# A gated mix of attention and a dense layer on one core: four two-reading sets whose sum GpSimd makes, eleven tiles of powers, and a new order

## The chip, the cores and the metric

The kernel runs on one core of one Trainium2 chip. A core has a matrix engine (TensorE, PE in the profile), a vector engine (VectorE, DVE), an engine for activation functions (ScalarE, ACT), a programmable engine (GpSimd, POOL) and SyncE (SP), which here only issues transfers between the DRAM and the core's on-chip memory. Each engine runs its own instructions in order, and they wait for each other by semaphores. The metric is the time of one execution on the device, in microseconds (us); less is better.

## The reference

`x` is 2048 rows of 640 values in bf16. A gate g is computed for each row, and the result mixes an attention `a` over 32 heads of 20 values and a dense layer `b`, both of the shape of x:

```python
x = A_x
g = _sigmoid((x * gate_w).sum(-1, keepdims=True))
# a: q, k, v = x @ wqkv in 32 heads; softmax(q k^T / sqrt(20)) v; @ wo
a = _A_ref(x, A_wqkv, A_wo)
# b: h = x @ w1 + b1 (1536 wide); h * tanh(softplus(h)); @ w2
b = _B_ref(x, B_w1, B_b1, B_w2)
return g * a + (1 - g) * b
```

The bulk is the softmax: 32 heads x 2048 x 2048 scores, each of which needs an exponential, and a product with the values.

## The kernel before, in words

**Groups.** The heads are taken four at a time (8 head groups p), the queries 512 at a time (4 chunks qc): 32 groups G. In each group the 2048 keys are 16 tiles j of 128, and a tile has four units, one for each head. A unit's scores are one matmul that uses 32 rows of PE (`score`, L1074), so four units of different heads can run at the same time; they fill one bank of PSUM, the accumulator memory of eight banks. Seven banks hold scores and other results, the eighth (`acc`) gathers the products with the values.

**Two ways to an exponential.** Of most tiles ACT makes the exponentials (`emit_exp`, L1092), mostly of two banks at once. Of 167 tiles, here called sets, DVE makes powers instead: `power_of` (L587) multiplies a bank's scores, adds a constant and writes 16-bit integers, whose bits read as bf16 are a rough exponential, into a quarter of a tile `T` of 128x2048. The roughness is averaged out by several readings of the same powers: GpSimd adds a constant to every 16-bit integer (`add_shift`, L617, an INT64_ADD that treats four of them as one word), which makes another tile, and the value product is made with each reading.

- An ordinary set (`d_shifts`) has three readings: T and two shifted ones. PE makes three value steps `V j,0`, `V j,1`, `V j,2` with them, the second and third with values scaled beforehand (`VD`).
- A two-reading set (`d_sum`) has a shifted tile, to which T is added (`total`, L641), and T shifted in place (`again`). PE makes two value steps. Six sets of the kernel before are of this kind, and DVE makes their sum.

T tiles have numbered places, T0 to T8 before: nine tiles for powers and shifted ones.

**The dense work.** Projections, the layer b and the product with wo are `Chain`s of column matmuls (`product`, L664), cut in pieces. Weights of the q and k projections come in strips (`load_strip`, L433), w1 in pairs of columns (`load_w1`, L446). The attended rows go to DRAM and come back transposed as `od` (`load_o`, L924). Twice ACT runs Mish over half of b's hidden values (`mish`, L872) for 10.4 us; PE works on chains in that time.

**The order.** Nothing is scheduled when the kernel is built. A string, `ORDER`, lists 5820 steps, and the loop at the end of the kernel emits them one by one; an engine's order is that in which its instructions come from the string. The letters that matter here:

- `S n,k`: n units of scores for ACT into banks k and on; `x n`: the exponential of n of these banks
- `d G,tag,two`: a set of group G is taken from the end of its keys, its T at place tag; `two` says of which kind it is
- `D G,j,r,k`: scores of unit r of the set (G, j) into bank k; `y n`: the n-th of DVE's waiting steps, a power, a copy out of PSUM or a sum
- `p n,tag`: the n-th of POOL's waiting steps, its output at place tag (-1: none, or in place)
- `V j,i`: the value step of key tile j with reading i (-1: ACT's exponentials), of the group that is being gathered
- `C`, `F`: begin a chain, make its next piece; `H`: filler matmuls; `q`, `k`, `b`, `o`, `l`: transfers on SP's queue; `m`: Mish

POOL's steps are numbered when they become known: a set's shifts once its last power is emitted.

Of the kernel before, what the change touches and what calls it, by code (L numbers as in the profile page):

```python
# [19 lines left out]
C0,4 S2,5 S2,2 S2,0 x2 x2 F F F F F C1,5 F y1 y3 C2,6 F x2 y4 C3,5 S2,2 F x2 y5 S2,0 C4,6 F x2 y2 y6 S2,2 C6,5  # L20
x2 F F F F F F F F F F F F F F F F F F F F C5,6 F F S2,0 S2,3 F F F x2 y7 y8 y9 x2 y10 y11 y12 C7,2 F F F F F
S2,0 x2 S2,5 C8,3 F F F F F F F F F F F F F F d1,3,0 V0,-1 F F F F F F V1,-1 y13 y14 y15 x2 C9,4 S3,0 F F F F
S2,5 F x3 x2 y16 y17 y18 y19 C10,6 V2,-1 S3,1 V4,-1 V3,-1 S2,4 V5,-1 F F F F F x3 x2 y20 C11,5 S3,0 d0,8,0 F F
d1,1,0 F F F F F F F F F F D0,15,3,4 D0,15,0,3 F F F F F F F F C12,6 V6,-1 x3 S3,0 F F F F y21 y23 y24 d0,0,0
y22 y25 y26 y27 x3 S2,3 D0,15,2,5 F x2 y28 y29 S3,0 C13,5 V7,-1 F F S2,3 D0,14,3,6 F F F x2 q1 y30 y31 x1 x2
C14,0 V9,-1 S2,1 D0,15,1,6 F F F F F F F F F D0,14,0,3 S2,4 F F F V8,-1 y32 x2 q2 y33 x2 D0,14,1,6 S2,1 F F F
F F F F F y34 x2 y35 C15,6 V10,-1 S3,3 y36 y37 y38 y39 F F F F F F D0,14,2,2 v0,0 S2,0 V15,0 F F F F V11,-1 x3
y41 y42 y40 p1,2 x2 D1,15,1,5 S3,2 y43 y44 x3 V14,0 V15,1 y45 D1,15,0,6 y46 C16,5 S2,0 V12,-1 F F F F F F
d1,2,0 D1,15,2,6 S3,2 p3,4 p4,7 p2,6 l0 y47 F V14,1 F F F V13,-1 x2 x3 D1,14,0,6 S2,0 d2,5,0 y48 y49 y50 V14,2
V15,2 C17,5 F x2 D1,15,3,4 S2,2 d1,0,0 y51 l1 F F x2 y52 D1,14,1,6 S2,0 d2,4,0 F F x2 p5,6 S2,2 D1,14,2,4 x2  # L30
p6,8 y54 y55 y56 l2 V0,-1 V1,-1 C18,5 S2,0 D1,13,0,6 F F F x2 y57 y53 y58 S3,2 F F S2,0 D1,13,1,6 V15,0 V2,-1
V15,2 V15,1 x3 y59 l3 y60 x2 D1,12,0,5 y61 C19,6 S3,2 F F F F F F V3,-1 S2,0 D1,14,3,5 F d2,6,0 F F F x3 y62
V4,-1 S3,2 x2 l4 y63 p7,7 y64 q3 x1 x2 C21,2 V5,-1 V14,0 D1,13,3,6 S2,0 D2,15,0,5 F F F F p8,8 y65 y66 x2
D1,13,2,6 S2,3 l5 y67 V14,1 F x2 D1,12,3,5 S2,0 y68 p9,3 V14,2 V13,0 V6,-1 x2 y69 D1,12,2,6 S3,2 p10,1 y70 x1
l6 x2 C20,2 V7,-1 V13,1 d3,7,0 D1,12,1,5 S2,0 y71 x2 F F F F F F F F F D2,15,3,6 S3,3 F V12,0 V13,2 V8,-1
p11,3 y72 x3 l7 p12,8 y73 V12,1 S2,0 D2,15,1,6 y74 y75 x2 C22,2 V9,-1 F F D2,14,0,3 S2,4 F F F F D2,15,2,6
S2,0 F F F F y76 x2 l8 y77 x2 y78 S2,3 y79 x2 C23,6 D2,14,3,5 V12,2 F F V10,-1 D2,14,1,0 S2,1 F V11,-1 F y80
p13,3 d2,2,1 y81 x2 l9 y82 S2,3 D2,13,0,5 F F F F F S2,0 D2,14,2,2 F p14,0 x2 y84 x2 y83 y85 V15,2 S2,4
D2,13,3,3 V15,1 V0,-1 D2,13,1,2 S2,0 p15,8 x2 e0 p16,3 x2 y86 y87 y89 y90 e2 V1,-1 V15,0 C24,2 V14,0 V14,1
S2,3 D2,12,0,5 F F S2,0 D2,13,2,6 F F x2 y91 x2 D2,12,3,5 S2,3 d2,1,0 x2 y92 y93 p17,8 V2,-1 d3,0,0 F S2,0  # L40
D2,12,1,6 V3,-1 V13,0 V14,2 y94 x2 p18,5 y95 D2,11,0,4 S2,2 x2 C25,5 V13,1 F S2,0 D2,12,2,6 F F y96 y88 y97 x2
D2,11,3,4 S2,2 F F p19,4 y98 x2 S2,0 D2,11,1,6 y99 x2 y101 V4,-1 V13,2 S2,2 d3,3,0 C26,5 D3,15,0,4 F F F S2,0
D2,11,2,6 F V6,-1 y102 x2 S2,2 D3,15,3,4 F V5,-1 y100 x2 y103 y105 x2 p20,-1 q4 S2,0 V12,0 V7,-1 x2 y104
d3,8,0 p21,6 D3,14,0,6 S2,2 D3,14,3,5 V11,0 V12,1 y106 x2 S2,0 D3,15,1,4 p22,5 y107 x2 y108 V11,1 C27,5 V8,-1
D3,13,0,6 S2,2 F F F F F D3,15,2,4 S2,0 F F F F F y109 x2 y110 k1 x2 D3,13,3,6 S2,2 x2 y111 d3,6,0 y113 p23,2
y112 V11,2 V9,-1 S2,0 D3,14,1,4 V10,-1 C29,6 x2 d3,4,0 y114 F F S2,2 D3,12,0,5 F F p24,1 y115 x2 D3,14,2,4
S2,0 V15,0 F y116 x2 d4,5,0 y117 y118 y119 S2,2 D3,12,3,5 V15,1 V0,-1 p25,7 x2 S2,0 D3,13,1,4 y121 y122 V14,0
V15,2 D3,11,0,6 S2,2 V14,1 V1,-1 x2 p26,2 y123 x2 D3,13,2,5 D3,12,1,4 S2,0 y120 y124 x2 V14,2 V2,-1 C28,6 F F
F F F F F q5 y125 S2,2 D3,11,3,5 p27,2 S2,0 y126 x2 F F F p28,1 y127 x2 y128 v1,0 V3,-1 V13,1 V13,0 C30,6 S3,2
D3,10,0,5 F F F F F x1 x2 y130 y131 y129 y132 D3,10,3,5 S3,0 x1 d4,2,0 x2 C34,0 d4,0,0 V4,-1 V13,2 V5,-1 S2,3  # L50
D3,12,2,6 F F F y133 y134 x2 D4,15,0,5 S2,1 p29,7 y135 F F x2 y136 p30,3 V12,0 S2,3 D3,11,1,6 V6,-1 V12,1 x2
y137 S3,0 D3,11,2,5 V12,2 x1 y138 S2,3 D3,10,2,6 x2 y139 C31,0 d4,1,0 V7,-1 F v2,0 F F d5,7,0 p31,8 x2 S2,1
D3,10,1,6 D4,14,0,5 q6 p32,3 x2 V11,0 F S2,3 F V8,-1 V11,1 y143 y142 p33,6 x2 y144 D4,15,1,6 S2,1 D4,13,0,5
V10,0 V11,2 p34,8 y145 x2 S2,3 D4,15,2,0 y146 x2 y147 C32,5 V9,-1 V10,1 D4,14,1,6 S2,1 F V10,2 y148 x2 S2,3
D4,15,3,0 F F S2,1 D4,13,1,6 F F y149 x2 y150 x2 p35,6 S2,3 D4,14,2,0 V0,-1 V15,0 V1,-1 y151 y152 y154 x2 S2,1
D4,12,0,6 p36,3 x2 y155 y153 C33,5 F d4,4,0 V2,-1 F S2,3 D4,14,3,0 x2 V15,2 V15,1 S2,1 D4,12,1,6 F F F x2 y141
y157 y140 p37,8 D4,13,2,0 S2,3 V3,-1 V14,0 y158 y160 y159 x2 S2,1 D4,11,0,6 p38,5 y161 y156 x2 C35,0 V14,1
V4,-1 D4,13,3,5 S2,3 F F F y162 x2 d5,6,0 D4,11,1,6 S2,1 F F p39,3 y163 x2 S2,3 D4,12,2,5 y164 V5,-1 V14,2
p40,8 x2 S2,1 D5,15,0,6 y165 V6,-1 V13,1 y166 x2 D4,12,3,0 S3,3 y167 C36,6 V13,0 F F F D4,11,2,2 S2,0 F F x3
p41,5 y168 x2 p42,3 d5,2,0 y169 V13,2 C37,2 S3,3 F F S2,0 D4,11,3,6 V12,1 F F x3 x2 y170 p43,0 D5,15,1,5 S2,3  # L60
F V12,2 V11,0 V7,-1 x2 y171 y172 p44,8 S2,5 D5,15,3,0 D5,15,2,1 V9,-1 V11,1 S3,2 V10,-1 V12,0 V8,-1 V11,2 x2
# [8 lines left out]
D6,14,3,5 V9,-1 V10,-1 F x2 y205 S2,2 D6,13,1,6 V11,-1 S2,0 D6,13,2,5 F F F x2 y206 y207 x2 d6,8,0 S2,2  # L70
D6,12,0,6 F y208 V15,0 S2,0 D6,13,3,5 V15,1 V14,0 x2 y209 y211 y210 y212 p54,2 p55,4 p56,6 x2 S2,3 D6,12,1,2
V14,1 V1,-1 V15,2 d6,2,0 S2,0 D6,12,2,6 V13,0 V0,-1 x2 p57,3 y214 y215 x2 S3,3 D6,11,1,2 y216 x3 C46,6 V14,2
V13,1 V2,-1 F D6,12,3,2 S2,0 F F D6,11,2,5 S2,3 x2 y213 y217 y218 F F p58,3 p59,7 x2 S2,0 D6,11,0,2 y219 x2
p60,4 V3,-1 V12,0 C47,5 F d6,1,0 y220 S2,3 D6,10,1,6 F F F D6,11,3,2 S2,0 F V13,2 x2 y221 y222 x2 S2,3
# [235 lines left out]
def kernel(  # L310
# [12 lines left out]
    nc = tc.nc  # L323
# [1074 lines left out]
```

## Time and profile before

| | us |
|---|---|
| median of 3 runs | 684.99 (684.69 to 685.27) |
| the profiled execution | 685.22 |
| its span, first to last instruction | 683.3 |
| PE busy | 674.1 |
| ACT busy | 667.3 |
| DVE busy | 594.2 |
| POOL busy | 354.2 |

The granted clock of PE is full throughout. A line of the groups' view reads: line of the kernel, engine, operation, output and inputs with their shapes, count | busy time in us, mean ns of one | idle time of the engine just before them, and what ended it. Busy times are unions of intervals that can overlap (matmuls and activations are pipelined), so a price of one step is better read from the starts in a timeline, whose lines have start, duration, engine, line and operation, and in brackets the idle time before and what ended it. `POOLq`, `SPq` and so on are the engines' sequencers.

### The profile page before, as it was taken

How to read it: one execution, taken by the hardware profiler on the slowest of the kernel's cores; microseconds unless marked ns; L12 is line 12 of the kernel's file. 1: busy time of each engine (PE TensorE's matmuls, PEld its weight loads, DVE VectorE, ACT ScalarE, POOL GpSimd, SP SyncE). 2: the span in 40 equal slices, each digit the busy share in tenths (PEclk: the TensorE clock that was granted, in tenths of full speed). 3: DMA queues.
4: the chain of work that ended last, by engine and by line, in shares of the span. 5: the costliest groups of instructions: out<-in, count | busy, mean ns of one | idle time of the engine just before them, and what ended most of it. 6: DMA issues, size and time to landing. Idle time of an engine off the chain costs nothing.

```text
span 683.3 us, 24544 instructions
## 1 busy us (share of the span) xinstructions
PE 674.1 (99%) x10379; PEld 234.7 (34%) x10379; DVE 594.2 (87%) x1027; ACT 667.3 (98%) x693; POOL 354.2 (52%) x349
## 2 busy tenths in 40 slices
PE   8999999999999999999999999999999999999997
PEld 4433233323323443333333223222243333333334
DVE  5689988898989879989878988999998988898896
ACT  6999999999999999999999999999999999999996
POOL 5045446454454535565545654456645655466543
PEclk9999999999999999999999999999999999999999
DMA  8454312212312211111231223321332121131221
GB/s 170 115 95 131 81 33 49 57 38 60 92 25 53 45 48 36 26 35 34 42 93 37 42 54 72 64 50 39 56 93 59 20 48 30 42 67 34 59 86 60
DMA packets 128542, 40.47 MB, mean 59 GB/s; under 512 B 94960, under 2 KB 127872, under 8 KB 128432
## 3 DMA queue, kind: packets, MB, share of 16 engines
q1 hardware_dynamic: 126032, 38.29, 25.3%
q8 instruction: 81, 1.33, 0.8%
q10 hardware_dynamic: 2400, 0.62, 0.4%
q14 instruction: 29, 0.24, 0.1%
HBM read 22.29 MB, written 12.78 MB: 51 GB/s over the span
## 4 chain that ended last, share of the span: by engine, by line
PE 81%; ACT 13%; issue 2%; DVE 2%; DMA 1%; POOL 0%; SPq 0%; ACTq 0%; POOLq 0%
PE Sp L1109 27%; PE Sp L1074 27%; PE Sp L664 26%; ACT E L1092 11%; ACT big L872 2%; DVE T L587 1%; DMA wf<-in_A_wqkv_dram 1%; PE Sp L1337 0%; DVE VD L569 0%; DMA q_dram<-st 0%; PE Sp L1218 0%; PE Sp L1124 0%; ACT L1092 0%; DVE ot L973 0%; POOL T L617 0%
## 5 line engine op out<-in xcount | busy, mean ns | idle before, releaser
L1092 ACT ACTIVATE E<-Sp 128x1024 bf16<-128x1024 f32 (+2 forms) x675 | 635.2, 1116 | 5.5 <-PE Sp L1074 4.3
L617 POOL INT64_ADD T<-T x334 | 344.3, 1042 | 315.5 <-DVE T L587 237.6
L587 DVE TENSOR_SCALAR T<-Sp 128x512 int16<-128x512 f32 x668 | 441.0, 683 | 59.4 <-PE Sp L1074 49.4
L1074 PE MATMUL Sp<-qT,kT 32*128 32x512 bf16 x2048 | 258.3, 384 | 3.4 <-ACT E L1092 1.1
L1074 PEld LDWEIGHTS <-kT 32*128 32x128 bf16 x2048 | 69.0, 91 | 244.7 <-issue 240.3
L1109 PE MATMUL Sp<-E,VA 128*21 128x512 bf16 x1380 | 130.5, 382 | 0.1
L1109 PE MATMUL Sp<-T,VD 128*21 128x512 bf16 x1312 | 119.6, 382 | 0.1
L664 PE MATMUL Sp<-w_sb,big 128*32 128x320 bf16 x1536 | 73.6, 302 | 0.0
L664 PE MATMUL Sp<-xT,w1t 128*32 128x512 bf16 x960 | 73.1, 383 | 0.0
L1109 PEld LDWEIGHTS <-VA 128*21 128x21 bf16 x2048 | 44.1, 90 | 58.9 <-issue 50.4
L1109 PE MATMUL Sp<-T,VA 128*21 128x512 bf16 x668 | 64.0, 382 | 0.0
L664 PE MATMUL Sp<-xT,ws 128*32 128x512 bf16 x720 | 52.9, 382 | 0.0
L1109 PEld LDWEIGHTS <-VD 128*21 128x21 bf16 x1312 | 31.0, 90 | 38.0 <-issue 30.9
L664 PEld LDWEIGHTS <-big 128*32 128x32 bf16 x1536 | 33.0, 95 | 29.0 <-issue 21.6
L851 DVE TENSOR_SCALAR big<-Sp,b1f 128x512 bf16<-128x512 f32 x48 | 35.6, 741 | 1.9 <-PE Sp L664 1.2
L664 PE MATMUL Sp<-wv,xT 128*32 128x81 bf16 (+2 forms) x960 | 31.6, 257 | 0.1
L664 PEld LDWEIGHTS <-w1t 128*32 128x32 bf16 x960 | 20.2, 95 | 26.0 <-issue 18.8
L664 PE MATMUL Sp<-wo_sb,od 128*32 128x320 bf16 (+1 forms) x608 | 27.2, 301 | 0.1
L753 DVE CAST st<-Sp 128x512 bf16<-128x512 f32 x36 | 24.6, 683 | 2.9 <-PE Sp L664 1.9
L1138 DVE STREAM_TRANSPOSE T<-Sp 128x512 f32<-128x512 f32 x32 | 22.7, 709 | 2.3 <-PE Sp L1109 2.2
L664 PEld LDWEIGHTS <-xT 128*32 128x32 bf16 x960 | 19.4, 96 | 10.8 <-issue 7.9
L664 PEld LDWEIGHTS <-ws 128*32 128x32 bf16 x720 | 15.5, 95 | 19.1 <-issue 12.1
(76 smaller groups left out, 191.8 us busy)
## 6 DMA issues: line engine op xcount, KB each, us to landing
w1t<-in_B_w_dram SPq DMA_DIRECT2D x24, 320.0 KB
q_dram<-st SPq DMA_DIRECT2D x20, 128.0 KB
b_dram<-bt SPq DMA_DIRECT2D x16, 160.0 KB
bl<-b_dram SPq DMA_DIRECT2D x16, 160.0 KB
qT<-q_dram SPq DMA_DIRECT2D x124, 20.0 KB
o_dram<-T SPq DMA_DIRECT2D x120, 20.0 KB
out_dram<-ot SPq DMA_DIRECT2D x15, 160.0 KB
kT<-k_dram SPq DMA_DIRECT2D x28, 80.0 KB
```

The source lines that it names most:

```text
L587: nc.vector.tensor_scalar(out=dst.bitcast(I16), in0=src, scalar1=inv_sqrt_dh * LOG2E * 128.0, scalar2=127.0 * 128.0 + (BETA2 if two else B ...
L617: nc.gpsimd.int64_add(dst[:, :].bitcast(I64), src[:, :].bitcast(I64), n * 0x0001000100010001)
L664: nc.tensor.matmul(out_[k : k + 32], lhsT=lhsT[:, k : k + 32], rhs=rhs, tile_position=(0, k), **kw)
L753: nc.vector.tensor_copy(out=res["st"][:, :], in_=ps[:, :])
L851: nc.vector.tensor_scalar(out=big[:, pair_of(c, ft), (ft % 2) * QC : (ft % 2 + 1) * QC], in0=ps[:, :], scalar1=b1f[:, ft : ft + 1], scalar ...
L872: nc.scalar.activation(v, v, ACT.Mish)
L1074: nc.tensor.matmul(ps_cols, lhsT=kT[p][32 * t_ : 32 * t_ + 32, j * P : (j + 1) * P], rhs=qT[G][32 * t_ : 32 * t_ + 32, :], tile_position=( ...
L1092: nc.scalar.activation(E[:, x : x + n, :], allb[:, k0 : k0 + n, :], ACT.Exp, scale=inv_sqrt_dh,)
L1109: nc.tensor.matmul(acc[32 * t_ : 32 * t_ + DH + 1, :], lhsT=lhsT, rhs=rhs, start=(pv_done[G] == 0), stop=(pv_done[G] == pv_total[G] - 1), ...
L1138: nc.vector.transpose(out=st["T1"][:, :, :].rearrange("p b r -> p (b r)"), in_=acc[:, :])
```

## The change

Three things change.

1. A third kind of set. `two` = 2 marks a two-reading set whose sum GpSimd makes: the addition becomes a step of POOL, and DVE has no part in it. The new order has four of these, all of which were ordinary sets: set 15 of group 1 (`d1,1,2`), sets 14 and 13 of group 23 (`d23,2,2`, `d23,10,2`) and set 15 of group 29 (`d29,6,2`). The six sets summed by DVE stay.
2. Eleven places for T tiles, T0 to T10. Their room comes from the strips and w1's pairs, which had tiles of their own and are now slices of the two tiles that the gated rows `od` have later in the kernel; one strip, the fifth of q, gets a tile of its own.
3. All of `ORDER` is new. It has as many steps as before, with 836 V where there were 840 and 338 p where there were 334.

```diff
 ORDER = """
...
-S2,0 x2 S2,5 C8,3 F F F F F F F F F F F F F F d1,3,0 V0,-1 F F F F F F V1,-1 y13 y14 y15 x2 C9,4 S3,0 F F F F
+F F F F F S2,0 x2 C8,3 S2,5 V0,-1 d1,1,2 F F d0,7,0 F F F F F F F F F F F F F F F F F F y13 y14 y15 x2 V1,-1
...
+y60 x2 D1,12,0,5 y61 C19,6 S3,2 V3,-1 F F F F F F D1,14,3,5 S2,0 F F F F x3 y62 S3,2 x2 l4 y63 p6,-1 p9,-1
...
+S2,2 V14,0 d23,2,2 V15,2 p226,0 x2 S2,0 D22,12,0,4 p227,6 y696 y697 d22,1,0 y698 x2 C128,5 F F D22,12,2,6 S2,2
...
+D22,11,1,4 y704 y705 d23,10,2 p230,9 x2 y706 C129,5 V5,-1 V14,1 F S2,2 D22,10,2,6 F D22,10,0,4 S2,0 F F F x2
...
+S2,3 F F x2 y733 S2,0 D23,11,0,5 F o0,4,5 y734 x2 D23,13,3,4 S2,2 y735 x2 F F D23,11,1,5 S2,0 y736 p241,-1
...
+y751 b5 p243,-1 p244,-1 C147,3 F F F F F C162,6 F F F F F V11,0 V14,1 D24,15,0,0 D23,10,3,2 D24,15,1,1 y752
+y755 q27 C148,3 S2,4 F F F F F C150,2 F F F F F V13,0 V14,0 V12,0 V9,-1 p245,4 p249,-1 p247,2 p246,5 p250,1
+p251,3 p248,-1 y753 y756 y757 y754 y758 V11,1 V12,1 V13,1 D24,15,3,0 D24,15,2,3 y759 y760 x2 H V8,-1 V10,0
...
+F F D27,15,2,4 S2,2 x2 p284,9 y844 y845 d29,6,2 x2 p285,1 F F d27,7,0 F D27,14,1,5 S2,0 F F F F y846 x2
...
+S2,1 C161,6 D29,12,3,5 F V8,-1 D29,13,2,0 S2,3 x2 y906 F F V10,-1 d31,1,0 S2,1 D29,11,0,5 F F p304,4 p307,-1
...
     strips = {}
+    strip_all = work.tile([P, 4, KT, P], BF16, tag="od0", name="ws")
     w1t = {}
+    w1_all = work.tile([P, 2, KT, 2 * P], BF16, tag="od1", name="w1t")
...
     def load_strip(kind, i, eng):

-        t = work.tile([P, KT, P], BF16, tag=f"ws{kind}_{i % 2}", name="ws")
+        if (kind, i) == (0, 4):
+            t = work.tile([P, KT, P], BF16, tag="ws", name="ws")
+        else:
+            t = strip_all[:, 2 * kind + i % 2]
...
-            w1t[k] = work.tile([P, KT, W1N * P], BF16, tag=f"w1t{k % 2}", name="w1t")
+            w1t[k] = w1_all[:, k % 2]
...
             add_shift(d[0], d["T"], SHIFT2[0])
-            dve(total, lambda: gps(again))
-
-        def total():
-            nc.vector.tensor_tensor(out=d[0][:, :], in0=d[0][:, :], in1=d["T"][:, :], op=ALU.add)
+            if d["two"] == 2:
+                gps(lambda k: total(nc.gpsimd), lambda: gps(again))
+            else:
+                dve(lambda: total(nc.vector), lambda: gps(again))
+
+        def total(eng):
+            eng.tensor_tensor(out=d[0][:, :], in0=d[0][:, :], in1=d["T"][:, :], op=ALU.add)
...
+    def pool(k, tag):
+        fn, done, _ = waiting["G"].pop(k)
+        fn(tag)
+        if done:
+            done()
...
-        "p": lambda k, tag: waiting["G"].pop(k)[0](tag),
+        "p": pool,
```

In the changed kernel the addition has line L649 and `add_shift` line L622.

More of the change, by code (lines that the diff above doesn't have):

```diff
@@ L25 @@
[L25 to L49, printed above, removed]
@@ L70 @@
[L70 to L74, printed above, removed]
@@ new lines @@
+V2,-1 S2,2 D13,13,3,4 x2 y437 V3,-1 V14,2 S2,0 D13,11,0,5 x2 x2 y435 y439 y438 y440 V14,0 C91,5 V4,-1
+D13,12,2,4 S2,2 V15,1 V14,1 D13,11,1,6 S2,0 F F F p134,3 x2 y441 d14,10,0 y442 d14,8,0 p135,0 x2 S2,2
+D13,12,3,4 F F y443 x2 D14,15,0,6 S2,0 V13,2 V13,1 V13,0 y444 p136,5 D13,11,3,5 S3,2 x2 y445 V5,-1 D13,11,2,6
+S2,0 p137,2 y446 x3 y447 x2 p138,4 q15 V6,-1 V7,-1 C92,5 V12,0 V12,2 F D14,14,0,6 S3,2 F F F F F F F y448
+p139,6 D14,15,2,6 S2,0 F F F F y449 d14,9,0 x3 x2 D14,15,1,2 S2,3 V11,1 V8,-1 S2,0 d15,2,0 D14,15,3,6 V12,1
@@ new lines @@
+p266,3 x2 V14,2 V15,1 S2,2 D25,11,0,5 y801 y802 x2 V13,0 V2,-1 S2,0 D25,11,2,6 V0,-1 V12,0 D25,11,1,4 S2,2
+V3,-1 V14,1 y803 y804 p267,8 p268,5 x2 d26,4,0 y805 S2,5 D25,11,3,1 D25,10,2,0 V13,2 V12,1 x2 x2 S2,2
+D25,10,0,4 p269,7 o1,0,4 y806 d26,1,0 y807 x2 p270,6 y808 V13,1 V4,-1 V12,2 D25,10,3,6 S2,0 V11,0 D25,10,1,5
+S3,2 x2 y809 y810 x3 V5,-1 V11,1 D26,15,0,6 C141,5 S2,0 p271,5 p272,6 p273,8 y811 x2 F F F F F F F S3,2
+D26,15,2,6 F F F F F V10,1 y812 x3 D26,15,1,6 S2,0 d26,7,0 V6,-1 V10,0 y813 y814 x2 d28,3,0 d26,9,0 S2,3
```

503 lines of the change are left out of this document (257 added, 246 removed).

## The prediction

> **What bounds the kernel now.** I read the page's busy times and chain first, then the groups by line with their shapes kept apart, then short stretches of the timeline, to get the price of one step from start to start (a matmul's busy time overlaps its neighbour's, so it is no price).
>
> ```profile
> PE 674.1 (99%) x10379; PEld 234.7 (34%) x10379; DVE 594.2 (87%) x1027; ACT 667.3 (98%) x693; POOL 354.2 (52%) x349
> PE 81%; ACT 13%; issue 2%; DVE 2%; DMA 1%; POOL 0%; SPq 0%; ACTq 0%; POOLq 0%
> L1092 ACT ACTIVATE E<-Sp 128x1024 bf16<-128x1024 f32 x581 | 552.6, 1097 | 4.6 <-PE Sp L1074 3.5 <-ACT E L1092 0.4 <-PE Sp L1109 0.2
> L617 POOL INT64_ADD T<-T x334 | 344.3, 1042 | 315.5 <-DVE T L587 237.6 <-PE Sp L1109 32.0 <-PE Sp L1074 23.8
> L587 DVE TENSOR_SCALAR T<-Sp 128x512 int16<-128x512 f32 x668 | 441.0, 683 | 59.4 <-PE Sp L1074 49.4
> L1074 PE MATMUL Sp<-qT,kT 32*128 32x512 bf16 x2048 | 258.3, 384 | 3.4 <-ACT E L1092 1.1 <-DVE T L587 0.9 <-DVE qT L1237 0.4
> L1109 PE MATMUL Sp<-T,VD 128*21 128x512 bf16 x1312 | 119.6, 382 | 0.1
> ...
> 299.51 25.38 ACT L1092 ACTIVATE E<-Sp 128x1024 bf16<-128x1024 f32 x28
> ```
>
> TensorE is the bound: 81% of the chain is PE, and its own groups show almost no idle time before them (3.4 us ahead of all 2048 score matmuls, 0.1 ahead of the value products with VD). ACT looks as full, but its exponentials overlap: the last row, from the timeline, has 28 of them in 25.38 us. With 1.10 us for the last, that is 0.90 us from start to start. At 0.90 each the 581 wide ones need 523 us of ACT, not 552.6, so ACT has room and waits for scores. POOL waits 315.5 us for powers that DVE has not made yet.
>
> The price of PE's steps, from two stretches of its timeline (start us, us, line, out<-in):
>
> ```profile
> 301.80 0.39 PE L1074 MATMUL Sp<-qT,kT 32*128 32x512 bf16 x3
> 302.12 0.62 PE L664 MATMUL Sp<-xT,ws 128*32 128x512 bf16 x8
> 302.67 0.39 PE L1074 MATMUL Sp<-qT,kT 32*128 32x512 bf16 x3
> ...
> 315.28 0.40 PE L1109 MATMUL Sp<-T,VA 128*21 128x512 bf16 x4
> 315.50 0.39 PE L1109 MATMUL Sp<-T,VD 128*21 128x512 bf16 x4
> 315.71 0.39 PE L1109 MATMUL Sp<-T,VA 128*21 128x512 bf16 x4
> 316.04 0.39 PE L1074 MATMUL Sp<-qT,kT 32*128 32x512 bf16 x4
> 316.36 0.40 PE L1109 MATMUL Sp<-T,VD 128*21 128x512 bf16 x4
> ```
>
> One value step (V, four matmuls side by side) costs 0.22 us to the next (315.28 to 315.50). A score step followed by column work costs 0.32, and the last column step before scores 0.33: each change between scores and column work adds 0.11.
>
> **The change part by part.** *PE work.* 836 V steps instead of 840, since each of the four sets is read twice and not three times: 4 x 0.22 = 0.9 us. In the new order the scores stand in 636 unbroken blocks where they stood in 642, so 12 changes of kind go: 12 x 0.11 = 1.3 us. They fill 648 steps of up to four row groups instead of 650: 2 x 0.22 = 0.4 us. All other work on PE, ACT and DVE is the same in number (668 powers, 6 DVE adds, 675 exponentials, 1220 chain pieces). Sum: 2.6 us off the engine that sets the end. Bounds: 0.9, if only the V steps count, and 2.6; I take 2.6, as PE's rows show no idle time that would swallow it.
>
> *Buffers.* w1 and the strips become slices of the gated rows' two tiles; loads stay at the same places of SP's queue, and each waits for the readers of its own slice as before. The gated rows come into that room at some 463 us of PE work (od0, last strip load at 303.7) and 530 (od1).
>
> ```profile
> L446 SPq DMA_DIRECT2D w1t<-in_B_w_dram x24: 368/402/1275, 43.2 to 478.0; - x24
> L433 SPq DMA_DIRECT2D ws<-in_A_wqkv_dram x9: 395/402/580, 10.8 to 303.7; - x9
> ```
>
> The last w1 load goes out at 478.0, over 50 us earlier than od1's first. Cost 0 on both sides; if a load waited for the wrong slice, a qT load queued on SP behind it would be late. Two more T tiles let DVE and POOL run further ahead; DVE's waits are for scores (49.4 of 59.4 us), so I give this nothing.
>
> *GpSimd's additions.* Four times POOL makes a shift, an addition of two tiles of 128x2048 and a second shift in place, where an ordinary set has two shifts. The addition has no row on POOL. It is also no INT64_ADD: in the changed program as built, POOL's stream has one more instruction without operands ahead of each addition (L649) and one behind it (L622). Before has a single such place, ahead of its first INT64_ADD, and its trace shows what it is: a change of POOL's code library.
>
> ```profile
> L617 POOLq MODIFY_POOL_CONFIG  x2: 6/6/6, 15.0 to 15.0; - x2
> 13.19 1.80 POOL L1245 MEMSET kT<- 128x2048 bf16 x1
> 30.77 0.68 DVE L587 TENSOR_SCALAR T<-Sp 128x512 int16<-128x512 f32 x1
> 31.55 1.04 POOL L617 INT64_ADD T<-T  x1 [16.57 <-DVE T L587]
> 0.73 0.39 SPq L459 DMA_DIRECT2D big<-in_A_x_dram  x1
> 3.73 0.16 PEld L1200 LDWEIGHTS <-big 128*128 128x128 bf16 x2 [0.70 <-DMA big<-in_A_x_dram]
> L872 ACT ACT_TABLE_LOAD x2 | 2.6, 1283 | 0.0
> L641 DVE TENSOR_TENSOR T<-T 128x2048 bf16<-128x2048 bf16 x6 | 7.3, 1213 | 0.0
> ```
>
> What a library change costs is not to be seen: POOL then idles 16.57 us, but for powers. So one change costs between 0 and 16.6 us. Three rows lie nearest: ACT's reload of a table already on its engine, 1.28 us; a first fetch from DRAM, issue at 0.73 to use at 3.73, 3.0 us; and two MODIFY_POOL_CONFIG for the one change, which makes 6.0 if each means a fetch. I take 6.0, since code for another library must come from outside the engine. For the addition: at least the 1.80 us in which POOL writes 2048 elements, at most three such streams (5.4); I take two, 3.6, the two inputs read in turn. A POOL addition with its two changes, c, is then 6.0 + 3.6 + 6.0 = 15.6 us, with ends of 1.8 and 38.6.
>
> The Trainium skill (GPSIMD Engine Reference, 2.1 Instruction dispatch) speaks against this change: the first call into a freshly loaded library pays about 6 us, which no row of the profile shows. The same page (3.1, Elementwise side by side) has 4497 ns for a two-input addition of 2048 fp32 elements on GpSimd. An estimate from that page is c = 16.4 us and, by the sum below, 725.6 us. No run here shows either figure yet; the 16.57 us gap has room for them.
>
> *Who waits.* POOL works in order, and so does PE: a late shift holds a V step, and every score and exponential behind it. How long c may be I read from the order, pricing PE's steps as above; the quickest way from a set's last score to its shift is 0.39 (the scores) + 0.68 (the power) + 0.1 (from 31.45 to 31.55) + 1.04 (the shift) = 2.2 us.
> - Set 15 of group 1: its last score at 38.4 us of PE work. POOL's queue: shift, addition, shift again, then set 14's first shift, which PE's V14,1 wants at 48.4. 10.0 - 2.2 - 2 x 1.04 leaves c at 5.7.
> - Sets 14 and 13 of group 23, in the second Mish stage: last score of the first at 479.5, and V11,2, which wants the seventh shift queued behind both additions, at 500.4. 20.9 - 2.2 - 9 x 1.04 leaves 9.3 for two c.
> - Set 15 of group 29: 595.2, and V14,1 at 606.0 wants the shift behind the addition: 10.8 - 2.2 - 1.04 leaves 7.6.
>
> At c = 15.6 PE waits 9.9 + (31.2 - 9.3) + 8.0 = 39.8 us. ACT and DVE, fed by PE, idle beside it, and nothing is queued elsewhere that could fill PE's place. At the lower end of c no wait arises.
>
> *Sum.* The profiled execution took 685.22 us (span 683.3, 1.9 around it), 0.2 above the median of 684.99. 685.2 - 2.6 + 39.8 = 722.4; **722 us**, 5.4% slower.
>
> **The rivals.** *Changing the library costs next to nothing* (both stay on the engine): c = 3.6, below every allowance, 685.2 - 2.6 = 682.6 us, faster. For it: the order's allowances, 4.65 to 7.6 us, suit an addition alone, and the first INT64_ADD starts 0.1 us after its powers. Against it: 16.5 us had passed since the change by then. It holds until the waits eat 2.6 us, at (c - 5.7) + (2c - 9.3) = 2.6, c = 5.9, or 1.1 us per change.
>
> *The change is like ACT's table load*, 1.28 us: c = 6.2, waits 0.5 + 3.1 = 3.6, 686.2 us, which is within 0.2% (about what a measurement of this kernel can tell from no change) or just over it. Against it: that table load has its data at hand.
>
> *The PE work saved is not the bound*: exponentials hold PE instead, and nothing happens, 685.2. Against it stand 0.90 us per exponential and the chain's 13% for ACT.
>
> *The new order brings waits of its own*: PE's rows have 3.4 us of idle time for 2048 scores; twice that would be 3.4 us more, 686.0. A bank is written again 1.92 us of PE work after the scores it held, in the median, in both orders, which speaks against it.
>
> **How the numbers follow.** Forecast (c of 8 us or more) 0.57; library free 0.33; like a table load 0.05, half of it within 0.2%; exponentials bind 0.02; waits of the order 0.03. Faster 0.33, same 0.05, slower 0.62. The forecast's own range: c of 8 gives 2.3 + 6.7 + 0.4 = 9.4 us of waits, 692; c of 17, with an addition of three streams (5.4) and changes of 5.8, gives 45.4, 728. Cases of both signs are likely, so the range goes from a little below the free library, 681.5, to 728; what lies above, up to the 38.6 us end of c, I leave out with 0.1.
>
> **What would show it.** MODIFY_POOL_CONFIG at nine places instead of one; POOL idle for some 6 us before each L649 addition and before the INT64_ADD behind it; PE idle at V14,1 near 57 us, in the second Mish stage from some 510 us and near 645 us, put down to POOL, 10, 22 and 8 us long. If the additions follow their shifts at once, the free library is right, and the span is about 681. If POOL idles and PE doesn't, my reading of the allowances is wrong. PE's busy time without waits should be 2.6 us smaller; DVE's adds stay 6 and V steps on VD fall from 1312 to 1296 matmuls.

## The result and the profile after

The changed kernel takes 738.44 us (median of 4 runs, 737.36 to 738.6), beside 685.12 us for the kernel before in the same series (684.69 to 685.27). The ratio is 1.0765, with a 95% interval of 1.0748 to 1.0783. The forecast of 722 us had the sign and the cause, but the loss is 53 us where it said 37.

The rows of the page after that answer to those shown of before (busy times, two of the rows of 40 slices, the chain, groups):

```profile
PE 684.5 (93%) x10363; PEld 236.7 (32%) x10363; DVE 594.4 (81%) x1027; ACT 669.2 (91%) x693; POOL 370.2 (50%) x353
...
PE   8976999999999999999999999999629999986997
...
PEclk9997999999999999999999999999858999996999
...
PE 71%; ACT 14%; issue 8%; POOL 4%; DVE 3%; DVEq 0%; POOLq 0%; ACTq 0%
...
L1100 ACT ACTIVATE E<-Sp 128x1024 bf16<-128x1024 f32 (+2 forms) x675 | 637.1, 1108 | 52.2 <-PE Sp L1082 51.5
...
L1117 PE MATMUL Sp<-T,VD 128*21 128x512 bf16 x1296 | 122.0, 390 | 34.7 <-POOL T L622 34.7
...
L1117 PE MATMUL Sp<-T,VA 128*21 128x512 bf16 x668 | 65.9, 394 | 6.5 <-POOL T L649 6.5
...
L649 POOL TENSOR_TENSOR T<-T 128x2048 bf16<-128x2048 bf16 x4 | 16.2, 4048 | 28.0 <-issue 28.0
```

PE's value products with VD had 0.1 us of idle time before them; now they have 34.7, and those with VA have 6.5, all put down to POOL. The exponentials, which are fed by PE, wait 52.2 us for scores. In the chain PE's share falls from 81% to 71%, POOL's rises from 0 to 4% and that of "issue", waiting for nothing that the profile shows, from 2% to 8%. The PE row shows three dents, in slices 3 and 4, 29 and 30, and 36 and 37. The granted clock, the part of its full speed at which TensorE is let run, falls there too (slices 4, 29 to 31, and 37), and that was not in the prediction.

GpSimd's timeline at the four additions, in three stretches, with the instruction's start and duration in us and in brackets the idle time before it:

```profile
41.75 1.04 POOL L622 INT64_ADD T<-T  x1 [3.85 <-DVE T L592]
49.66 4.05 POOL L649 TENSOR_TENSOR T<-T 128x2048 bf16<-128x2048 bf16 x1 [6.87 <-issue]
59.67 5.09 POOL L622 INT64_ADD T<-T  x5 [5.96 <-issue]
...
519.66 4.07 POOL L649 TENSOR_TENSOR T<-T 128x2048 bf16<-128x2048 bf16 x1 [7.34 <-issue]
529.81 2.05 POOL L622 INT64_ADD T<-T  x2 [6.08 <-issue]
538.69 4.03 POOL L649 TENSOR_TENSOR T<-T 128x2048 bf16<-128x2048 bf16 x1 [6.83 <-issue]
548.67 9.14 POOL L622 INT64_ADD T<-T  x9 [5.95 <-issue]
...
659.11 4.04 POOL L649 TENSOR_TENSOR T<-T 128x2048 bf16<-128x2048 bf16 x1 [7.00 <-issue]
668.93 4.08 POOL L622 INT64_ADD T<-T  x4 [5.79 <-issue]
```

Each addition is 4.05 us long. GpSimd stands still for 6.8 to 7.3 us ahead of it and for 5.8 to 6.1 us behind it, waiting for nothing that the profile shows ("issue"). The first addition thus keeps GpSimd from its shifts for 6.87 + 4.05 + 5.96 = 16.9 us. The groups by source line, asked for L649 and for L622, show what is issued there:

```profile
L649 POOLq MODIFY_POOL_CONFIG  x8: 1/11/11, 42.7 to 652.2; - x8
L622 POOLq MODIFY_POOL_CONFIG  x10: 1/2/7, 15.2 to 663.4; - x10
```

That is two for each of nine changes of library, four of them ahead of an addition, and five ahead of an INT64_ADD.

What PE does at the first of these places (its timeline):

```profile
50.91 0.39 PE L1082 MATMUL Sp<-qT,kT 32*128 32x512 bf16 x3
61.77 0.61 PE L1117 MATMUL Sp<-T,VD 128*21 128x512 bf16 x4 [10.47 <-POOL T L622]
...
63.28 0.61 PE L1117 MATMUL Sp<-E,VA 128*21 128x512 bf16 x4
63.67 0.64 PE L1117 MATMUL Sp<-T,VD 128*21 128x512 bf16 x4
...
67.54 0.40 PE L1117 MATMUL Sp<-T,VA 128*21 128x512 bf16 x4
67.77 0.39 PE L1117 MATMUL Sp<-T,VD 128*21 128x512 bf16 x4
```

It waits 10.47 us for a shift. After that a value step takes 0.39 to the next start (63.28 to 63.67), and some four microseconds later 0.22 again (67.54 to 67.77, rounded). The view by windows has the clock (columns: stretch, its length, busy us and instructions of PE, PEld, DVE, ACT and POOL, the granted clock, the DMA share and GB/s):

```profile
50.00:62.00 12.00, 1.53 (x25) 0.58 (x27) 1.96 (x3) 2.63 (x3) 6.04 (x4) 0.70 0.31 90
62.00:70.00 8.00, 8.00 (x120) 2.54 (x116) 4.69 (x8) 5.71 (x6) 4.81 (x5) 0.80 0.58 181
530.00:575.00 45.00, 29.42 (x405) 10.55 (x404) 20.80 (x34) 19.23 (x21) 23.84 (x21) 0.74 0.08 18
575.00:660.00 85.00, 84.64 (x1350) 30.50 (x1347) 74.15 (x127) 84.98 (x89) 44.38 (x44) 1.00 0.22 41
660.00:690.00 30.00, 20.07 (x285) 6.11 (x282) 14.83 (x24) 18.18 (x19) 17.07 (x15) 0.77 0.19 43
```

Finer stretches of the same trace have the clock at 1.00 up to 54.91 us and at 0.50 from there to 65.15: it falls 3.6 us into the wait and is still at half for the first 3.4 us of work behind it. So the change has two costs: PE waits for GpSimd, and PE then works at half speed. The Trainium skill (TensorE: Matmul & The Clock Gate, Part 1) says that an idle window of about 3.4 us brings half rate, and a busy one of that length full rate again; the rows above agree with that, but further down waits of 2.1 to 2.2 us brought half rate too.

### The profile page after: what moved, and what is told of

The parts are those of the page before. It is cut to its first block, busy times and chain, and to the rows that moved or that the text cites. A ratio compares the mean times of both kernels' runs of the same rounds, so it can differ in the third digit from the quotient of the medians.

```text
span 736.8 us, 24508 instructions
## 1 busy us (share of the span) xinstructions
PE 684.5 (93%) x10363; PEld 236.7 (32%) x10363; DVE 594.4 (81%) x1027; ACT 669.2 (91%) x693; POOL 370.2 (50%) x353
## 4 chain that ended last, share of the span: by engine, by line
PE 71%; ACT 14%; issue 8%; POOL 4%; DVE 3%; DVEq 0%; POOLq 0%; ACTq 0%
PE Sp L1117 24%; PE Sp L1082 23%; PE Sp L672 22%; ACT E L1100 12%; POOL T L622 2%; POOL T L649 2%; ACT big L880 1%; DVE T L592 1%; PE Sp L1351 0%; PE Sp L521 0%; DVE T L1160 0%; PE Sp L1132 0%; PE Sp L1226 0%; DVE ot L981 0%; ACT L1100 0%
## 5 line engine op out<-in xcount | busy, mean ns | idle before, releaser
L1100 ACT ACTIVATE E<-Sp 128x1024 bf16<-128x1024 f32 (+2 forms) x675 | 637.1, 1108 | 52.2 <-PE Sp L1082 51.5
L622 POOL INT64_ADD T<-T x334 | 344.1, 1042 | 324.1 <-DVE T L592 223.8
L1082 PE MATMUL Sp<-qT,kT 32*128 32x512 bf16 x2048 | 261.6, 387 | 4.4 <-ACT E L1100 2.2
L1117 PE MATMUL Sp<-T,VD 128*21 128x512 bf16 x1296 | 122.0, 390 | 34.7 <-POOL T L622 34.7
L1117 PE MATMUL Sp<-T,VA 128*21 128x512 bf16 x668 | 65.9, 394 | 6.5 <-POOL T L649 6.5
L1117 PEld LDWEIGHTS <-VA 128*21 128x21 bf16 x2048 | 44.7, 91 | 67.2 <-issue 58.3
L649 POOL TENSOR_TENSOR T<-T 128x2048 bf16<-128x2048 bf16 x4 | 16.2, 4048 | 28.0 <-issue 28.0
L672 PEld LDWEIGHTS <-w1t 128*32 128x32 bf16 x960 | 20.2, 95 | 26.1 <-issue 17.9
```

Source lines behind the costliest of these rows:

```text
L622: nc.gpsimd.int64_add(dst[:, :].bitcast(I64), src[:, :].bitcast(I64), n * 0x0001000100010001)
L649: eng.tensor_tensor(out=d[0][:, :], in0=d[0][:, :], in1=d["T"][:, :], op=ALU.add)
L672: nc.tensor.matmul(out_[k : k + 32], lhsT=lhsT[:, k : k + 32], rhs=rhs, tile_position=(0, k), **kw)
L1082: nc.tensor.matmul(ps_cols, lhsT=kT[p][32 * t_ : 32 * t_ + 32, j * P : (j + 1) * P], rhs=qT[G][32 * t_ : 32 * t_ + 32, :], tile_position=( ...
L1100: nc.scalar.activation(E[:, x : x + n, :], allb[:, k0 : k0 + n, :], ACT.Exp, scale=inv_sqrt_dh,)
L1117: nc.tensor.matmul(acc[32 * t_ : 32 * t_ + DH + 1, :], lhsT=lhsT, rhs=rhs, start=(pv_done[G] == 0), stop=(pv_done[G] == pv_total[G] - 1), ...
```

## The experiments

All times are medians, and the ratio to the kernel before was measured on the same chip in the same series. The kernel before came out between 685.9 and 686.8 us in these series.

**The additions replaced by short shifts.** The theory is that a library change keeps GpSimd away and PE waits for it; the rival is that the new order itself is slow. In `total`, for GpSimd (the sum is left out):

```diff
         def total(eng):
+            if eng is nc.gpsimd:
+                for _ in range(4):
+                    add_shift(d[0], d[0], 0)
+                return
             eng.tensor_tensor(out=d[0][:, :], in0=d[0][:, :], in1=d["T"][:, :], op=ALU.add)
```

> The four additions on GpSimd are replaced by four INT64_ADDs in place each (4 x 1.04 = 4.2 us against the addition's own 4.05), so the order, the buffers and POOL's work stay and only the eight library changes go. It leaves the sum out: the four sets are read as if T had not been added. Theory (the library changes cause the waits): c = 4.2 is below the allowances 4.65 to 7.6, no waits, 685.2 - 2.6 = 682.6 us, within 681.5 to 684. Rival (the new order or the shared room costs time of its own): 690 us or more, since 53 us would have to come from elsewhere than the library.

Measured: 688.02 us (687.43 to 691.14), ratio 1.0029 (1.0012 to 1.0046). Some 50 of the 53 us are gone, so they come from GpSimd's part and not from the new order or the buffers. But the order brings no gain: the time ends above the kernel before, not 2.6 us below. In its groups the products with VD no longer wait:

```profile
L1121 PE MATMUL Sp<-T,VD 128*21 128x512 bf16 x1296 | 119.5, 382 | 0.0
```

The four shifts in place took 4.5 us (42.46 to 46.99), within the 4.65 us and more that the prediction read from the order. As this kernel and the changed one issue the same matmuls in the same order, their starts can be subtracted one by one. The changed kernel falls behind only at the waits and in the steps right after them:

| wait ends at (us) | wait adds | slow steps after it add |
|---|---|---|
| 61.77 (V14,1, group 1) | 10.5 | 1.5 |
| 531.91 (V14,1, group 23) | 7.3 | 1.8 |
| 542.77 (V13,0, group 23) | 6.8 | 0.6 |
| 551.79 (V11,1, group 23) | 7.6 | 2.3 |
| 670.02 (V14,1, group 29) | 10.0 | 2.4 |
| sum (before rounding) | 42.3 | 8.6 |

Between these places the distance stays constant within 0.1 us. The sum, 50.9 us, and 0.4 us at the start are the whole 51.2 us between the two profiled executions (687.43 and 738.6).

**Sixteen shifts.** If only GpSimd's absence counts, 16 shifts of 1.04 us must cost what an addition with its two library changes costs (16.9 us). The edit is the one above with `range(16)`; the sum is left out.

> As with four INT64_ADDs in place, but sixteen: c = 16 x 1.04 = 16.6 us without a library change, close to the 16.9 us (6.9 idle, 4.05 addition, 6.0 idle) of the changed kernel. It leaves the sum out. Theory (what counts is only how long POOL is away): waits and slow clock as in the changed kernel, 735 to 739 us. Rival (a library change also disturbs the other engines, by its transfers or by holding the sequencer): clearly less, 720 us or below.

Measured: 743.0 us (742.78 to 745.02), ratio 1.0829 (1.0795 to 1.0863). Without any library change the waits and the fall of the clock are there again (the clock is 0.65 from 62 to 70 us). The time lies above the 735 to 739 us expected, because the stand-in was too long: in place the shifts follow each other at 1.14 us, not 1.04, so that the next shift starts 19.3 us after the one ahead of the sixteen (41.79 to 61.09), where it was 17.9 in the changed kernel (41.75 to 59.67). PE's first wait is longer by the same 1.4 us:

```profile
63.20 0.61 PE L1121 MATMUL Sp<-T,VD 128*21 128x512 bf16 x4 [11.86 <-POOL T L622]
```

So an absence of GpSimd of that length is enough for all of the loss. And as the starts in the table above keep their distance between the five places, nothing shows a library change disturbing PE or ACT by itself; what it costs is time on GpSimd's queue.

**An addition that is almost nothing.** The library changes stay, but the addition has 16 columns of 2048.

```diff
         def total(eng):
-            eng.tensor_tensor(out=d[0][:, :], in0=d[0][:, :], in1=d["T"][:, :], op=ALU.add)
+            n = 16 if eng is nc.gpsimd else 4 * QC
+            eng.tensor_tensor(out=d[0][:, 0:n], in0=d[0][:, 0:n], in1=d["T"][:, 0:n], op=ALU.add)
```

> Each of the four GpSimd additions is done on 16 columns of 2048 only, so nearly all of the sum is left out; the library changes around it stay. If what counts is the time for which GpSimd is away from the shifts, each absence is shorter by nearly the 4.05 us of the addition: the waits of 42.3 us become 42.3 - 4 x 3.8 = 27, the half clock after them stays, and the time is 738.4 - 15 = 723 us (721 to 726). Rival: the idle time around the addition is a fixed pause that only partly lies beside it, and grows when the addition is short: 730 us or more.

Measured: 724.71 us (723.71 to 725.21), ratio 1.0549 (1.0525 to 1.0572), 13.7 us less than with whole additions. GpSimd's timeline at the first and the last of the four:

```profile
51.80 0.20 POOL L650 TENSOR_TENSOR T<-T 128x16 bf16<-128x16 bf16 x1 [7.73 <-issue]
58.24 4.08 POOL L622 INT64_ADD T<-T  x4 [6.24 <-issue]
...
649.58 0.20 POOL L650 TENSOR_TENSOR T<-T 128x16 bf16<-128x16 bf16 x1 [7.04 <-issue]
655.78 6.10 POOL L622 INT64_ADD T<-T  x6 [6.00 <-issue]
```

The addition is down to 0.20 us; the two changes still take 14.0 and 13.0 us. So with the library changes in place the additions themselves account for some 14 of the 53 us. The two parts do not simply add up: four shifts of about an addition's length cost PE no wait in the first experiment, as they stayed within what the order leaves.

**One addition alone.** `total` takes the path with four shifts except where `d["G"] == 29`; three sums are left out.

> Only the set of group 29 is added by GpSimd; in the other three sets four shifts of 1 us stand in the addition's place, without a library change, and their sums are left out. By the theory the costs add place by place: the 688.0 us of the run with all four replaced, 10.0 us for the wait near 670 us, and about 2 us for the half clock after it: 700 us (698 to 703), with one half-clock stretch and one POOL idle pair of some 6.9 and 5.9 us. Rival: the first library change of a run alone is dear, or later ones get cheaper: the time differs from 700 by over 3 us.

Measured: 700.49 us (698.22 to 704.31), ratio 1.0207 (1.0176 to 1.0237). The timelines of GpSimd and PE at the one place left:

```profile
619.68 4.04 POOL L653 TENSOR_TENSOR T<-T 128x2048 bf16<-128x2048 bf16 x1 [6.99 <-issue]
629.71 7.35 POOL L622 INT64_ADD T<-T  x7 [5.99 <-issue]
...
630.79 0.61 PE L1121 MATMUL Sp<-T,VD 128*21 128x512 bf16 x4 [10.11 <-POOL T L622]
```

The time is 12.5 us above that of the kernel with four shifts everywhere, beside 12.4 us for this place in the table. The costs add place by place, and the first pair of library changes ahead of an addition is as dear here as the fourth pair was in the changed kernel.

**The sums on VectorE.** Nothing is left out; the additions stand at the same steps, on DVE.

```diff
-            eng.tensor_tensor(out=d[0][:, :], in0=d[0][:, :], in1=d["T"][:, :], op=ALU.add)
+            nc.vector.tensor_tensor(out=d[0][:, :], in0=d[0][:, :], in1=d["T"][:, :], op=ALU.add)
```

> The changed kernel with the four sums on VectorE, at the same steps of the order; nothing is left out. Theory: no library change and no addition on POOL, four DVE adds of 1.21 us more; DVE has 59 us of waits for scores to hide 4.9 us in, so 682.6 us, within 681.5 to 684.5, faster than before. Rival (DVE, in order, waits for POOL's shift at these steps and holds the powers behind it): up to 2 us for each set, 690 us.

Measured: 693.61 us (692.38 to 696.78), ratio 1.0110 (1.0078 to 1.0142). The four additions take 1.21, 1.70, 1.21 and 1.22 us there, and PE no longer waits for GpSimd, but the time stays above that of the kernel before. Right behind the four additions (at 49.5, 504.6, 515.8 and 623.4 us) PE waits for powers and copies of DVE, 0.46, 1.40, 1.00 and 0.58 us long, and the kernel with four shifts has none of these waits; another 1.1 us goes to a transfer of qT at 36 us. That is the rival of the expectation, DVE holding its other work back, for 3.4 of some 5.6 us. Of the kernels that compute the whole, none beat it.

**The buffers alone.** The kernel before, with only the strips and w1 in the room of the gated rows:

```diff
+    strip_all = work.tile([P, 4, KT, P], BF16, tag="od0", name="ws")
+    w1_all = work.tile([P, 2, KT, 2 * P], BF16, tag="od1", name="w1t")
...
-        t = work.tile([P, KT, P], BF16, tag=f"ws{kind}_{i % 2}", name="ws")
+        if (kind, i) == (0, 4):
+            t = work.tile([P, KT, P], BF16, tag="ws", name="ws")
+        else:
+            t = strip_all[:, 2 * kind + i % 2]
...
-            w1t[k] = work.tile([P, KT, W1N * P], BF16, tag=f"w1t{k % 2}", name="w1t")
+            w1t[k] = w1_all[:, k % 2]
```

> The kernel before with its strips and w1 buffers put into the room of the gated rows, and with nothing else of the change: same order, ten buffers of powers. Theory: the sharing costs nothing, since the strips are used before the first gated rows: 685 us, ratio within 0.2% of 1. Rival: the shared room makes a late strip or w1 load wait on a first gated row, or a gated row on it: over 686.5 us, with PE waiting on a DMA.

Measured: 686.14 us (684.96 to 689.65), ratio 0.9999 (0.9983 to 1.0015). The sharing costs nothing. (This kernel has the nine places for T tiles of the kernel before, not the ten of the expectation.)

**Spare matmuls in the waits.** If the half clock costs time of its own, matmuls that keep PE busy through the waits must win it back. First in the changed kernel, with 175 groups of `H` ahead of the five steps that wait (all of the computation is done):

```diff
-V14,1 F x2 S2,0 D1,12,3,5 y68 p8,4 p10,8 V6,-1 V14,2 V13,0 x2 y69 S3,2 D1,12,2,6 p11,5 y70 x1 l6 x2 V7,-1
+H H H H H H H H H H H H H H H H H H H H H H H H H H H H H H H H H H H H H H H H H H H H V14,1 F x2 S2,0 D1,12,3,5 y68
...
```

> The changed kernel with 175 filler matmul groups (H, zero weights into acc) ahead of the five value steps at which PE waits, 0.22 us each, somewhat less than each wait; nothing is left out. Theory (after each wait PE runs at a granted clock of 0.5 for some us, and that is the part of the 53 us that the waits, 42 us, do not explain): the clock stays 1.0 and the time falls by about 9 us, to 729 us, 727 to 732. Rival (the slow clock falls into time that PE has anyway, and the rest comes from the order): 738 us, or more by the filler.

Measured: 737.11 us (734.41 to 739.85), ratio 1.0737 (1.0699 to 1.0775): almost no gain. GpSimd's timeline at the first place shows one reason:

```profile
42.42 1.04 POOL L622 INT64_ADD T<-T  x1 [4.94 <-DVE T L592]
50.95 4.07 POOL L649 TENSOR_TENSOR T<-T 128x2048 bf16<-128x2048 bf16 x1 [7.50 <-issue]
61.71 5.09 POOL L622 INT64_ADD T<-T  x5 [6.69 <-issue]
```

GpSimd's chain began 0.7 us later here, and its pauses were 7.50 and 6.69 us, where they were 6.87 and 5.96. (Only the second of them lies beside the spare matmuls, which begin at 51.90 us.) PE's first wait therefore ends 2.0 us later, at 63.81 us, and longer pauses of GpSimd hide what the clock may win: it is at half for 6.8 us in all around the waits, where it was for 47.8. So the test was clouded by the library changes, and was made again without them: sixteen shifts for each addition (the sum left out), with the same 175 groups.

> Sixteen shifts of 1 us in place of each of the four additions (no library change; the sum is left out), and ahead of the five waiting PV steps the 175 groups of spare matmuls, which keep TensorE busy while it would wait. The run with sixteen shifts and no spare matmuls took 743.0 us, with 54.9 us of half clock as the sum of its four stretches. Theory: the half clock after a wait costs some 9 us, and the spare matmuls take it away while they add nothing of their own, as they run in the wait: 734 us (732 to 737), the granted clock at full speed in all four places. Rival: the clock's fall costs nothing that counts, the steps after a wait being bound by something else: 743 us.

Measured: 744.82 us (743.59 to 746.67), ratio 1.0849 (1.0824 to 1.0873), no gain in the total. PE's timeline at the first place and the clock of three stretches:

```profile
51.53 9.68 PE L1136 MATMUL Sp<-xT,zero_w 128*21 128x512 bf16 x176
63.42 0.40 PE L1121 MATMUL Sp<-T,VD 128*21 128x512 bf16 x4 [2.22 <-POOL T L622]
...
62.00:70.00 8.00, 6.58 (x116) 2.64 (x115) 4.68 (x8) 5.54 (x6) 6.47 (x7) 1.00 0.44 113
530.00:575.00 45.00, 34.03 (x583) 14.75 (x575) 15.04 (x26) 13.38 (x14) 33.00 (x33) 0.89 0.08 18
660.00:690.00 30.00, 27.88 (x472) 10.51 (x460) 16.38 (x28) 18.84 (x20) 26.16 (x26) 1.00 0.11 20
```

The clock stays full at the first and the last place; it is at half for 10.2 us in all, beside 51.2 us in the run with sixteen shifts alone (the expectation has 54.9). The starts, subtracted from those of the kernel with sixteen shifts alone, fall back by 1.9 us after the first wait, 1.6 after V11,1 of group 23 and 2.0 after the last: 5.5 us won. The 1.8 us won after the wait near 533 us are lost again at the next wait, because GpSimd's chain still ends when it did. And 6.0 us were lost where the spare matmuls ahead of V11,1 ran longer than the wait there. So the theory holds place by place where the clock stayed full, and the total hid it. To see it in the total, those 31 groups were moved to V13,0, where 9.6 us of wait had stayed uncovered:

> As the run with sixteen shifts and 175 groups of spare matmuls (744.8 us, no library change, the sum left out), but the 31 groups that stood ahead of V11,1 near 552 us, where they ran 6 us longer than the wait, now stand ahead of V13,0, whose wait of 9.6 us was left uncovered. Theory: the overrun of 6 us goes, and with it the last half-clock stretch, worth 1 to 2 us: 737 us (735 to 739), against 743.0 without any spare matmuls, so that the half clock after the waits costs some 6 to 8 us in all. Rival: spare matmuls are no cheaper than the waits and the half clock: 742 us or more.

Measured: 741.64 us (740.68 to 743.57), ratio 1.0818 (1.0800 to 1.0837). The overrun is gone, but only some 1.5 us of the half clock were won, as it came back at places where the run before had kept it away:

```profile
62.63 0.40 PE L1121 MATMUL Sp<-T,VD 128*21 128x512 bf16 x4 [2.23 <-POOL T L622]
...
62.00:70.00 8.00, 7.37 (x109) 2.47 (x112) 4.20 (x8) 4.86 (x6) 5.67 (x6) 0.79 0.52 141
```

With the same spare matmuls and the same wait left over (2.22 and 2.23 us) the clock fell in one run and not in the other. The traces suggest what decides it. In each of them the clock changes only at points that lie whole multiples of 3.413 us apart (in the changed kernel it is at half for 3, 2, 5 and 4 times that). Here the wait, from 60.40 to 62.63 us, lies whole between two such points, 59.56 and 62.97, and the clock is at half from 62.97 to 66.38. In the run before, the wait from 61.20 to 63.42 is cut by such a point at 62.39, counted back from 543.67, into 1.19 and 1.03 us, and the clock stays full. The last place agrees: 2.06 us in one piece here and half clock, 1.67 and 0.39 us there and full clock. No run moved a wait against these points on purpose, and how much idle time between two of them is enough stayed open: in the run with the short additions 1.5 us (between 648.63 and 652.05) were followed by half clock, and 1.9 us (between 522.34 and 525.75) were not.

**Why the new order gains nothing.** Three kernels ask where the 2.6 us of saved PE work went. Adding up the times from one matmul's start to the next, by the kinds of the two, the score steps inside unbroken blocks take 12.0 us in before and 17.6 in the kernel with four shifts, which is more than what the other kinds save (score step to column or value work 202.7 to 200.6 us, value step to score step 110.4 to 107.8). The steps among column and value work, which hold the four V steps fewer, take 270.9 us where they took 269.5. The PE timeline of the kernel with four shifts has places where a block stops; the second row waits for a bank inside a block:

```profile
501.77 0.65 PE L1086 MATMUL Sp<-qT,kT 32*128 32x512 bf16 x4
502.73 0.39 PE L1086 MATMUL Sp<-qT,kT 32*128 32x512 bf16 x2 [0.31 <-ACT E L1104]
```

The first test moves one or two steps of other work ahead of the waiting step at eight such places (two of them, cut out of their lines of the order; the sum is left out, as in the kernel with four shifts):

```diff
-C10,6 S3,0 d2,0,0 S2,3 V2,-1 V3,-1 V4,-1
+C10,6 V2,-1 V3,-1 S3,0 d2,0,0 S2,3 V4,-1
...
-D23,12,2,4 S2,2 y737 y738 x2 V6,-1 C134,4 V7,-1
+D23,12,2,4 V6,-1 V7,-1 S2,2 y737 y738 x2 C134,4
```

> As the run with four shifts in place of each addition (the sum left out), but at eight places where a score step waited for its bank inside an unbroken block of scores (0.43 to 0.94 us from start to start, 5.2 us together), one or two steps of other work that stood right behind the block are moved ahead of the waiting step. Theory: the new order loses what its fewer changes of kind were to gain because its longer blocks wait for banks; the waits go for the most part (some 4 us), eight changes of kind come back (8 x 0.11 = 0.9 us): 3 us less than the same kernel without the moves, 684.5 to 685.5 where that has 688. Rival: the exponentials set the pace, and a wait that is covered at one place comes back at the next: no change, 688 us.

> The run with four shifts of 1 us in place of each of GpSimd's additions once more (no library change, the sum left out), beside the one with the eight moves: 688 us, 0.3% above the kernel before, as it was.

Measured: 689.18 us (687.2 to 690.06), ratio 1.0036 (1.0023 to 1.0048) with the moves; 687.89 us (686.85 to 689.38), ratio 1.0032 (1.0020 to 1.0045) without. The steps inside blocks fell from 18.8 to 15.4 us in the profiled executions, but those from a score step to column or value work rose from 200.6 to 202.6, and the time did not move. The waits inside blocks thus look like a place where the loss shows, not like its cause.

The second test leaves out a quarter of the exponentials in both orders (the last 128 of a bank's 512 columns hold zeros instead); in the new order it has the four shifts, and the sum is left out too:

```diff
-            E[:, x : x + n, :], allb[:, k0 : k0 + n, :], ACT.Exp, scale=inv_sqrt_dh,
+            E[:, x : x + n, 0:384], allb[:, k0 : k0 + n, 0:384], ACT.Exp, scale=inv_sqrt_dh,
```

> The kernel before with each exponential made of 384 of a bank's 512 columns (the last 128 hold zeros, so a quarter of the exponentials is left out): ACT is about a quarter of its time lighter. If TensorE's own work is the bound, as the prediction has it, only the few waits for exponentials go: 681 us (679 to 684). If exponentials hold TensorE, more goes: below 678 us.

> The new order with four shifts of 1 us in place of each of GpSimd's additions (the sum left out) and the same shortened exponentials (a quarter left out). If it was the exponentials that ate the new order's smaller work on TensorE, that work now shows: 2.6 us less than the old order with shortened exponentials, ratio to that 0.996. If the new order's waits are for powers, copies or GpSimd, it stays 1.5 to 2.5 us slower than the old order, ratio 1.002 to 1.004.

Measured: the old order 679.73 us (679.49 to 680.45), ratio to the kernel before 0.9906 (0.9891 to 0.9921); the new order 680.65 us (679.38 to 682.42), ratio 0.9914 (0.9896 to 0.9931). The busy rows of the two:

```profile
PE 668.3 (98%) x10379; PEld 230.3 (34%) x10379; DVE 594.8 (88%) x1028; ACT 577.3 (85%) x693; POOL 354.0 (52%) x349
```

```profile
PE 668.6 (98%) x10363; PEld 230.3 (34%) x10363; DVE 592.8 (87%) x1028; ACT 577.0 (85%) x693; POOL 371.2 (55%) x365
```

With 90 us less on ACT the times fall by 6 to 7 us only, so PE is the bound, as the prediction had it. The new order is now 0.1% behind the old one instead of 0.3%, with intervals that overlap; the steps inside its blocks take 11.6 us against 8.5. About half of what it loses there goes with the shorter exponentials. The rest stands before banks that DVE frees (copies and powers) or is not explained. Neither expectation, 0.996 or 1.002 and more, was met, and this part stays open.

## Why the prediction went wrong, by its own steps

- *GpSimd's additions bring two changes of library each, and PE waits for them.* Right. The nine places, the idle time ahead of each addition and behind it, and the waits of PE in groups 1, 23 and 29 are all there; in group 23 PE stopped at V14,1, V13,0 and V11,1, ahead of the V11,2 that was named. The Trainium skill (GPSIMD Engine Reference, 2.1 Instruction dispatch) has about 6 us for the first call after a load; the trace of the changed kernel shows 6.8 to 7.3 us one way and 5.8 to 6.1 the other, at all four additions.
- *c = 15.6 us.* The term was too small: 6.87 + 4.05 + 5.96 = 16.9 measured. The two streams taken for the addition (3.6) came close to 4.05; the change into the addition's library was 0.9 us dearer than the 6.0 taken. By the prediction's own sum a c of 16.9 gives 45.0 us of waits, 5.2 more than forecast.
- *Who waits.* The allowances of 5.7, 9.3 and 7.6 us were right to about 1 us each. With the measured absences they give 16.9 - 5.7 = 11.2 us in group 1 (measured 10.5), 17.5 + 16.8 - 9.3 = 25.0 in group 23 (21.7, and 24.1 with the slow steps between its three waits, which run beside the same chain of GpSimd) and 16.8 - 7.6 = 9.2 in group 29 (10.0). Waits of 39.8 us were forecast, 42.3 were measured, and 44.7 with those slow steps. (Of GpSimd's 315.5 us of idle time in the kernel before, which the prediction puts down to powers, the row has 237.6 for them; that does not enter the sum.)
- *Nothing follows a wait.* This step failed, and the prediction did not state it: PE was taken to go on at its old price. It goes on at half clock. The slow steps after the waits add 8.6 us, of which 2.4 lie in group 23 where the next wait takes them up; 6.2 us count. The first run with spare matmuls and without library changes shows the same size from the other side, 5.5 us won at three places; in no total could this be seen.
- *PE work, -2.6 us, bounds 0.9 and 2.6.* This failed too. With GpSimd made cheap the new order is 0.3% slower, by 2.2 us in the profiled executions (687.43 against 685.22), and not 2.6 faster; PE's busy time, which was to be 2.6 us smaller, is 675.3 us there beside 674.1. The sentence that PE's rows show no idle time to swallow the gain was the error: those rows count idle time of PE, while the loss is in longer intervals between score steps. The rival in which the order brings waits of its own had it at 686.0, with a chance of 0.03; that it is exponentials that hold PE is at most half of it, and the rest of the cause stays open.
- *Buffers at no cost.* Right, by the run with the sharing alone. That the two additional tiles of powers give nothing was not tried by itself.
- *The sum.* 722.4 + 4.9 (waits 44.7, not 39.8) + 6.2 (half clock) + 4.8 (+2.2, not -2.6) = 738.3, beside 738.6 for the profiled execution.
- *The range* ended at 728, for a c of 17 with the saved work kept and the full clock. That c was nearly the one measured; the two failed steps lay outside it.
- *The library change is free*, the main rival, at 682.6: wrong by the idle time at all four additions. Its condition, c below 5.9, was far from met, and the order's own loss would have kept even a free change from that time: the kernel with four shifts shows 688.

## What to carry to other kernels

Keep GpSimd to instructions of one library in a stretch where anyone waits for it: an instruction of another library in between cost 13 us in changes there and back, every time, and the addition itself only 4. When a wait of some microseconds is put on TensorE, add to it the half clock that follows, here 1.5 to 2.4 us at each place, unless the next wait takes it up. And a count of saved steps on the busiest engine is an upper bound until the intervals between its steps, not its idle time alone, show that nothing else fills them.

## What the runs showed of the hardware

- A change of GpSimd's library took 6.8 to 7.3 us into the addition's and 5.8 to 6.1 us back to the shift's in the changed kernel, the last no cheaper than the first. With the addition on 16 columns it was 7.0 to 7.7 and 5.9 to 6.2 us, and with spare matmuls on TensorE 6.9 to 7.6 and 6.4 to 7.0 us.
- GpSimd added two tiles of 128x2048 in bf16 in 4.05 us, DVE in 1.16 to 1.22 us and once in 1.70.
- In the changed kernel, after idle times of 6.5 us and more, TensorE's granted clock was at half for 3.4 to 6.1 us of work, unless the next wait came first. A left-over wait of 2.2 us, behind 9.7 us of spare matmuls, brought it to half in two runs and not in a third.
- The granted clock changed only at points whole multiples of 3.413 us apart, in all of these traces. The 2.2 us waits that lay whole between two such points were followed by half clock for 3.41 us, and the one that was cut by such a point was not.
